# Query projections by row halves from the eighth score on, and three smaller moves of order, in a fused attention and feed-forward block

## The chip, the core and the metric

The kernel runs on one core of one Trainium2 chip. The metric is the device time of one execution in microseconds (us), as the median of several runs.

## What is computed

The reference, cut to its core (one sequence of S = 2048 rows, D = 512, H = 32 heads of 16 columns that share one key and one value head, F = 1792):

```python
def _A_ref(x, wq, wk, wv, wo):
    q = (x @ wq).reshape(B, S, H, Dh).transpose(0, 2, 1, 3)
    k = x @ wk
    v = x @ wv
    scores = jnp.einsum("bhqd,bkd->bhqk", q, k) * (Dh ** -0.5)
    p = _softmax(scores, axis=-1)
    o = jnp.einsum("bhqk,bkd->bhqd", p, v)
    return o.transpose(0, 2, 1, 3).reshape(B, S, H * Dh) @ wo

def _B_ref(x, w_gate, w_up, w_down):
    return (_gelu(x @ w_gate) * (x @ w_up)) @ w_down

h  = x + _A_ref(_layernorm(x), wq, wk, wv, wo)
h2 = h + _B_ref(_layernorm(h), w_gate, w_up, w_down)
```

## The kernel before

**Precision.** Most products are made of three float32r products: both operands are split into a high part and the rest, and high x high, high x rest and rest x high are added in PSUM. A "split" is a cast on one engine and a subtraction on another (`split`, lines 113 to 118).

**Order of the work.** A prologue (line 1206 on) normalises and transposes x, projects keys and values, and makes the first queries. Then come four blocks of 512 queries. Each has eight groups of four heads, each group sixteen slices of 128 keys. A "score" (`score(n)`, line 1006) is two matmuls for two heads, into one of three PSUM buffers, and one exponential of 128 x 1024 on ScalarE (line 395); two scores make a pair, of which four matmuls (`weigh`, line 397) add the weighted values into `acc`. There are 256 scores a block, 1024 in all, counted by n. During block 1 the dense work (output projection, layer norm, feed-forward) of block 0 is woven between the scores, and so on; the dense work of block 3 is a tail without scores.

**What lies in block 0.** Beside the scores of block 0 run the query projections of the other blocks. `project_q(b, cs, ...)` (line 185) makes the queries of block b in chunks c of 128 columns, twelve matmuls each, then splits them (`qh`, `ql`), squares them (`qs`) and stores qh, ql, qh in device memory (`q_d`, line 238). There are two forms. The full form uses all 128 rows of TensorE. The form by halves uses rows 0 to 63 for all twelve terms and then rows 64 to 127: each half matmul runs beside one matmul of a score, which uses the other 64 rows (line 389). Between the two halves of a chunk VectorE reads one column of the bank, a "mark" (line 208), on which TensorE's next half waits. In the form before, the first 32 scores go with full matmuls (chunks 0 and 1 of block 1, and what the prologue left of block 0, `early_q`), taken by steps of three at n = 3, 5, 7 (RAMP) and at every fourth n from 11; from n = 32 on cycles of three scores go with 4 or 2 halves, by a fixed pattern of seven cycles. A chunk in HURRY is first copied out of PSUM (`pq_raw`), so that the bank is free before the split.

**The bound.** For each block the kernel computes a bound of the scores from the squares: a small matmul (`pqn`, line 249), a copy and a maximum on VectorE, four tiny instructions on GpSimd (`factors`, lines 259 to 268), then `m` on VectorE and its store to `q_d` (line 279). These last two steps wait in the list `after`, which `age` counts down once a cycle. At the end of block 0 `check_bound` stores the largest bounds in `b_d` (line 1445).

**GpSimd's other work.** `part_weights` loads the raw weights wo, w_gate, w_up and w_down in 46 parts, splits each on GpSimd, and stores it to device memory; its DMAs go through GpSimd's queue.

**The turn to block 1.** At n = 256 the pool `early`, which held projections and weight parts, is closed, and the pool `dense` takes its memory. At n = 260 `dense(0)` issues on SP's queue, in this order: two tiles of x (`xb`, line 621), four tiles of w1 (line 547), two tiles of wo (`load_wo`, line 561). `evacuate` then copies the last `acc` of block 0 to `oT` (line 412), stores it (`acc_d`, line 416), gathers it back turned (`oc`, line 425), takes reciprocals of the sums, multiplies and splits it (`o_hi`, `o_lo`, lines 439 to 454). The output projection `pp` (`duo`, line 587) needs wo and all four chunks of `o_hi`.

**Whose order is fixed.** In this part the instructions of TensorE, ScalarE, GpSimd, VectorE and SP all stand in the order in which the program emits them. Each engine works through its own list and waits at the head of it.

Of the kernel before, what the change touches and what calls it, by code (L numbers as in the profile page):

```python
# [19 lines left out]
P = 128  # L20
# [16 lines left out]
FULL_Q = 2  # L37

HURRY = ((0, 3), (1, 0), (1, 1))
# [11 lines left out]
def kernel(  # L51
# [104 lines left out]
    def run(outer, first):  # L156
# [28 lines left out]
        def project_q(b, cs, eng, col, halves=()):  # L185
# [4 lines left out]
            for c in cs:  # L190
# [6 lines left out]
                if c in halves:  # L197
                    for a in range(2):
                        rows = slice(64 * a, 64 * a + 64)
                        for n, (lhsT, rhs) in enumerate(terms):  # L200
                            yield a, partial(
                                nc.tensor.matmul, pq, lhsT[rows], rhs[rows],
                                start=(a == 0 and n == 0),
                                stop=(a == 1 and n == len(terms) - 1), skip_group_check=True,
                            )
                        if a == 0:
                            mark = eb.tile([P, 1], F32, tag="qmark", bufs=2, name=f"mark_{b}_{c}")
                            nc.vector.tensor_copy(mark, pq[:, :1])
                else:
                    for n, (lhsT, rhs) in enumerate(terms):  # L210
                        nc.tensor.matmul(  # L211
                            pq, lhsT, rhs, start=(n == 0), stop=(n == len(terms) - 1)
                        )
                        if n % 3 == 2 and (urgent or n < len(terms) - 1):
                            yield 3
# [26 lines left out]
                if c not in halves and (raw is None or b == 0):  # L242
                    yield 3

# [54 lines left out]
        def early_q():  # L299

            second = project_q(1, range(DC), nc.vector, 1, range(FULL_Q, DC))
            for _ in range(sum(RAMP.values())):
                yield next(second)

            next(q_rest)
            for _ in range(FULL_Q * DC - sum(RAMP.values())):
                yield next(second)
            yield from q_rest
            rest_q.append(second)
            rest_q.extend(project_q(b, range(DC), nc.vector, b, range(DC)) for b in range(2, NB))  # L310

        rest_q = []

        def half_q():
            for gen in rest_q:
                yield from gen
# [19 lines left out]
        def first_bound(qg):  # L336

            m = ms[0]
            for u in range(2):
                for a, eng in enumerate((nc.sync, nc.scalar)):  # L340
                    eng.dma_start(
                        qg[64 * a + 3 * DH : 64 * a + 3 * DH + 1, 2 * u + a, :].bitcast(F32),
                        m[2 * u + a : 2 * u + a + 1, :].bitcast(F32),
                    )
            hs = slice(0, FIRST_Q * HC)
            nc.sync.dma_start(q_d[hs, 3 * DH, :T].bitcast(F32), m[hs].bitcast(F32))

# [209 lines left out]
        def load_wo(b):  # L557

            for j in range(DC // 2):
                w = db.tile([P, 2, 2, D], F32R, tag="w2", bufs=W2, name=f"wo_{b}_{j}")  # L560
                nc.sync.dma_start(
# [52 lines left out]
        def dense(b, tail=False):  # L614
# [14 lines left out]
            if b == 0:  # L629
                load_wo(b)  # L630
                yield 0
# [404 lines left out]
        with tc.manual_schedule(engines={mybir.EngineType.SP, mybir.EngineType.DVE}):  # L1036
            parts, said = None, 3
            if first:
                work = early_q()
                parts = part_weights(early.enter_context(tc.tile_pool(name="parts", bufs=1)))  # L1040

            while n < 2 * KC:
                for _ in range(RAMP.get(n, n > 7 and n % 4 == 3) if first else 0):
                    next(work, 0)
                    age()
                score(n)
                n += 1
                if n % 4:
                    continue
                if len(pend) > 2:  # L1050
                    finish(len(pend) - 2)
                if parts is not None and n > 12 and n % 24:
                    next(parts, None)

            token, counts = None, iter(())
            if first:
                drain()
                work = half_q()
                token = next(work)
                counts = (k for _ in range(NB * DC) for k in (4, 2, 4, 2, 4, 4, 4))  # L1060

            for cycle in range((lead - n) // 3):
                age()
                rest = token == REST
                count = next(counts) if token is not None and not rest else 0
                for j in range(3):
                    if n == 2 * PER:
                        assert token is None
                        for _ in parts or ():
                            pass  # L1070
                        while after:
                            age()
# [4 lines left out]
                        db = late.enter_context(tc.tile_pool(name="dense", bufs=1))  # L1077
                    if 0 < j <= count // 2:
                        score(n, (token, next(work)))
                        if j < count // 2:  # L1080
                            token = next(work)
# [8 lines left out]
                ready = [e[2] for e in pend if e[5] < n - 2]  # L1090
                if KC - 1 in ready:
                    ready = ready[: ready.index(KC - 1) + 1]
                finish(len(ready))
                if count:
                    token = next(work, None)
                if outs:
                    take_out()
                if parts is not None and cycle % 7 % 2 == 0:
# [424 lines left out]
```

## Time and profile before

| | us |
|---|---|
| median of three runs | 1439.77 |
| lowest and highest of them | 1437.53, 1440.94 |
| the profiled execution, its own time | 1437.67 |
| span of its instructions | 1436.0 |
| TensorE busy (matmul) | 1400.2 |
| ScalarE busy | 1042.7 |
| VectorE busy | 541.4 |
| GpSimd busy | 231.9 |

The times of all engines below come from one profiled execution, in us from the start of its span. A row of a timeline gives the start, the length, the engine (PE is TensorE, ACT ScalarE, DVE VectorE, POOL GpSimd, SPq SP's queue), the line in the kernel, the operation, what is written and read, how many instructions are merged, and in brackets how long the engine was idle before, and what ended that. A row of a group gives the count, busy us, the mean of one in ns, and the idle time before. A row of waits gives who waited for whom: us in total, times, longest.

### The profile page before, as it was taken

What the parts mean: (1) busy time and instruction counts of PE and PEld (TensorE: products, weight loads), DVE (VectorE), ACT (ScalarE), POOL (GpSimd) and SP (SyncE); (2) the same over time, 40 slices, a digit from 0 to 9 for tenths busy, and PEclk for the clock granted to TensorE, in tenths of its full rate; (3) what the DMA queues carried; (4) which work ended last, traced back from release to release, by engine and by line L of the source; (5) the groups of instructions that cost most, each with busy time, mean ns of one, the idle gap of its engine ahead of it and who ended that gap; (6) DMA issues with size and microseconds to landing.
All of it is one profiled execution on the core that took longest, in us unless ns stands there. A gap on an engine that the chain in (4) does not pass through costs nothing.

```text
span 1436.0 us, 25546 instructions
## 1 busy us (share of the span) xinstructions
PE 1400.2 (98%) x10622; PEld 787.2 (55%) x10622; DVE 541.4 (38%) x974; ACT 1042.7 (73%) x1149; POOL 231.9 (16%) x330
## 2 busy tenths in 40 slices
PE   8999999997999999999999999999999999999998
PEld 7533333334555555555555555554555555557886
DVE  7412231212344242423343342423353242427665
ACT  7699999994778777777777777777787787773000
POOL 6476776730000000000000000000000000002000
PEclk9999999998999999999999999999999999999999
DMA  4567767753144241305243241324143240436551
GB/s 157 161 229 222 226 224 225 235 197 111 48 153 144 74 142 43 132 12 202 60 165 120 86 145 35 117 78 144 57 160 128 86 136 27 146 123 203 177 203 62
DMA packets 71004, 193.69 MB, mean 135 GB/s; under 512 B 9676, under 2 KB 9676, under 8 KB 70848
## 3 DMA queue, kind: packets, MB, share of 16 engines
q1 hardware_dynamic: 60376, 155.69, 32.5%
q0 software_dynamic: 10336, 36.18, 7.6%
q8 instruction: 85, 1.39, 0.4%
q14 instruction: 39, 0.32, 0.1%
q10 hardware_dynamic: 168, 0.10, 0.0%
HBM read 142.12 MB, written 49.55 MB: 133 GB/s over the span
## 4 chain that ended last, share of the span: by engine, by line
PE 87%; ACT 6%; DMA 2%; DVE 2%; issue 1%; SPq 1%; POOL 1%; ACTq 0%; DVEq 0%; POOLq 0%
PE acc L399 30%; PE s L391 19%; PE pu L911 9%; PE pg L911 8%; ACT p L395 6%; PE pd L911 5%; PE pd L587 3%; PE pd L609 3%; PE pg L609 3%; PE pu L609 3%; PE pp L587 2%; PE pq L389 1%; DMA acc_d<-oT 1%; PE pq L211 1%; PE pp L719 1%
## 5 line engine op out<-in xcount | busy, mean ns | idle before, releaser
L395 ACT ACTIVATE p<-s 128x1024 f32<-128x1024 f32 x1024 | 971.2, 1028 | 250.8 <-PE s L391 248.9
L399 PE MATMUL acc<-p,v_sb 128*32 128x512 f32 x4096 | 491.0, 599 | 0.0
L391 PE MATMUL s<-qg,kaug 50*128 50x512 f32 x1984 | 420.2, 426 | 7.6 <-ACT p L395 7.5
L391 PEld LDWEIGHTS s<-qg,kaug 50*128 50x128 f32 x1984 | 192.4, 184 | 254.4 <-ACT p L395 126.5
L399 PEld LDWEIGHTS acc<-p,v_sb 128*32 128x32 f32 x4096 | 112.4, 109 | 235.5 <-issue 230.8
L911 PE MATMUL pu<-x2h,w 64*128 64x512 f32 x672 | 212.2, 391 | 0.0
L911 PE MATMUL pg<-x2h,w 64*128 64x512 f32 x672 | 211.4, 391 | 0.3 <-DVE mark_pg L934 0.3
L911 PEld LDWEIGHTS pu<-x2h,w 64*128 64x128 f32 x672 | 115.9, 185 | 14.9
L911 PEld LDWEIGHTS pg<-x2h,w 64*128 64x128 f32 x672 | 116.0, 185 | 14.5 <-DVE g L785 0.7
L911 PE MATMUL pg<-x2l,w 64*128 64x512 f32 x336 | 122.0, 391 | 0.0
L911 PE MATMUL pu<-x2l,w 64*128 64x512 f32 x336 | 122.0, 391 | 0.0
L127 POOL TENSOR_SCALAR rstd<-mv 128x1 f32<-128x1 f32 x16 | 3.6, 224 | 692.7 <-DVE mv L125 692.6
L788 ACT ACTIVATE ga<-ga 128x512 f32<-128x512 f32 x56 | 35.3, 634 | 89.2 <-DVE ga L783 89.2
L911 PE MATMUL pd<-w,gh 64*128 64x512 f32 x384 | 81.1, 392 | 0.0
L853 DVE TENSOR_TENSOR h<-h,pd 128x512 f32<-128x512 f32 x48 | 31.9, 685 | 115.4 <-PE pd L911 66.3
L439 DVE RECIPROCAL oc<-oc 128x128 f32<-128x128 f32 x64 | 56.3, 921 | 40.4 <-DMA oc<-acc_d 35.5
L1150 DVE SCALAR_TENSOR_TENSOR ga<-ga,g 128x512 f32<-128x512 f32 x70 | 48.3, 691 | 52.7 <-ACT ga L788 51.6
L412 DVE COPY oT<-acc 128x512 f32<-128x512 f32 x32 | 22.1, 691 | 119.0 <-PE acc L399 118.8
L772 DVE COPY g<-pg 128x512 f32<-128x512 f32 x56 | 38.7, 692 | 63.1 <-PE pg L911 57.4
L911 PEld LDWEIGHTS pu<-x2l,w 64*128 64x128 f32 x336 | 58.0, 185 | 7.3
L911 PEld LDWEIGHTS pg<-x2l,w 64*128 64x128 f32 x336 | 58.0, 185 | 6.9
L785 DVE TENSOR_TENSOR g<-g,pu 128x512 f32<-128x512 f32 x56 | 38.3, 684 | 40.2 <-PE pu L911 30.2
(276 smaller groups left out, 1475.3 us busy)
## 6 DMA issues: line engine op xcount, KB each, us to landing
w<-w_d SPq DMA_DIRECT2D x112, 512.0 KB
w<-w_d SPq DMA_DIRECT2D x28, 1024.0 KB
qg<-q_d SPq DMA_DIRECT2D x48, 200.0 KB
q_d<-qh SPq DMA_DIRECT2D x32, 256.0 KB
wo<-wo_d SPq DMA_DIRECT2D x8, 1024.0 KB
acc_d<-oT SPq DMA_DIRECT2D x31, 256.0 KB
oc<-acc_d SPq DMA_DIRECT2D x124, 64.0 KB
w_d<-w_0b POOLq DMA_DIRECT2D x14, 512.0 KB, 4.5
```

Of the source, the lines that this page charges most:

```text
L391: nc.tensor.matmul(s[:, a, :], kaug[rows, kc * P : (kc + 1) * P], qg[rows, 2 * u + a, :], start=True, stop=True,)
L395: nc.scalar.activation(p[:, 2 * u : 2 * u + 2, :], s, AF.Exp, scale=SCALE)
L399: nc.tensor.matmul(acc[32 * j : 32 * j + 32, :], v_sb[:, kc, :], p[:, j, :], start=(kc == 0), stop=(kc == KC - 1), skip_group_check=True,)
L439: nc.vector.reciprocal(oc[:, 1, sl], oc[:, 1, sl])
L587: nc.tensor.matmul(banks[k], lhsT[rows], rhs[rows], start=(turn == 0 and i == 0), stop=(turn == 1 and i == n - 1), skip_group_check=True,)
L609: nc.tensor.matmul(bank, lhsT, rhs, start=(i == 0), stop=(i == len(ts) - 1))
L772: nc.vector.tensor_copy(g, pg)
L785: nc.vector.tensor_tensor(g, g, pu, op=ALU.mult)
L788: nc.scalar.activation(a, a, AF.Tanh, scale=GELU_A * GELU_C)
L853: nc.vector.tensor_tensor(hs[t], hs[t], pd, op=ALU.add)
L911: nc.tensor.matmul(e["bank"], lhsT[rows], rhs[rows], start=i == 0 and not e["both"], stop=last and e["both"], skip_group_check=True,)
L1150: (soon or lazy).pop(0)()
```

## The change

It has four parts.

- The phase with full matmuls ends at n = 8. Of the full form only 18 matmuls of block 1 remain (chunk 0 and half of chunk 1), at n = 3, 5 and 7. From n = 8 on all scores go in cycles of three, with halves beside the second and third score. A cycle takes four halves, or two when the cycle before ended with two weighted sums and the halves are of the upper rows, and never goes past a half's end. The rest of block 0's projection (`q_rest`: the split of chunk 3 and the bound) is emitted at the start of the halves and after chunk (1, 1). At most two pairs are weighed per cycle. Because halves need both row ranges, the first queries `qg` are loaded into both, by two more DMAs on SP behind the store of `m`. Chunk (1, 1) is not in HURRY any more.
- The split of a finished chunk is emitted within the cycle, right after its last half, before the weighted sums and the copy of `acc` that may follow.
- At n = 256 the entries of `after` are emitted before what is left of the weight parts; the parts come in two of three cycles from cycle 3 on.
- `load_wo(0)` is emitted at n = 256, right after the pool is opened, on GpSimd's queue.

The diff, cut:

```diff
-FULL_Q = 2
-HURRY = ((0, 3), (1, 0), (1, 1))
+FULL_STEPS = 18
+HURRY = ((0, 3), (1, 0))
+BREAK = (1, 1)
...
+                for a in range(2) if full <= last else ():
+                    if a or full:
+                        mark = eb.tile([P, 1], F32, tag="qmark", bufs=2, name=f"mark_{b}_{c}_{a}")
+                        nc.vector.tensor_copy(mark, pq[:, :1])
+                    rows = slice(64 * a, 64 * a + 64)
+                    for n, (lhsT, rhs) in list(enumerate(terms))[full:]:
+                        yield a, last - n, partial(nc.tensor.matmul, pq, lhsT[rows], rhs[rows], ...)
...
+        def later_q():
+            second = project_q(1, range(DC), nc.vector, 1, {0: 3 * DC, 1: FULL_STEPS - 3 * DC})
             for _ in range(sum(RAMP.values())):
                 yield next(second)
             next(q_rest)
+            for token in second:
+                if token == HOLD:
+                    yield REST
+                    for _ in q_rest:
+                        pass
+                else:
+                    yield token
+            for b in range(2, NB):
+                yield from project_q(b, range(DC), nc.vector, b, {})
...
             nc.sync.dma_start(q_d[hs, 3 * DH, :T].bitcast(F32), m[hs].bitcast(F32))
+            for a in range(2):
+                nc.sync.dma_start(
+                    qg[64 * a : 64 * a + KR, 1 - a :: 2, :].bitcast(F32),
+                    q_d.rearrange("h r s -> r h s")[:, 1 - a : 4 : 2, :T].bitcast(F32),
+                )
...
-                nc.sync.dma_start(
+                (nc.sync if b else nc.gpsimd).dma_start(
                     w.bitcast(F32),
                     wo_d[2 * j : 2 * j + 2].rearrange("c p i d -> p c i d").bitcast(F32),
...
-            if b == 0:
-                load_wo(b)
...
-            while n < 2 * KC:
-                for _ in range(RAMP.get(n, n > 7 and n % 4 == 3) if first else 0):
+            while n < 2 * PB - 2:
+                for _ in range(RAMP.get(n, 0) if first else 0):
...
-                count = next(counts) if token is not None and not rest else 0
+                count = 0
+                if token is not None and not rest:
+                    count = min(4 if ran < 2 or token[0] == 0 else 2, token[1] + 1)
                 for j in range(3):
                     if n == 2 * PER:
+                        while after:
+                            age()
                         for _ in parts or ():
                             pass
-                        while after:
-                            age()
...
                         db = late.enter_context(tc.tile_pool(name="dense", bufs=1))
+                        load_wo(0)
                     if 0 < j <= count // 2:
-                        score(n, (token, next(work)))
-                        if j < count // 2:
-                            token = next(work)
+                        tokens = token, next(work)
+                        score(n, [(lane, step) for lane, _, step in tokens])
+                        token = next(work, None)
...
-                ready = [e[2] for e in pend if e[5] < n - 2]
+                ready = [e[2] for e in pend if e[5] < n - 2][:2]
...
-                finish(len(ready))
-                if count:
-                    token = next(work, None)
+                ran = len(ready)
+                finish(ran)
...
-                if parts is not None and cycle % 7 % 2 == 0:
+                if parts is not None and cycle > 2 and cycle % 3 < 2:
                     next(parts, None)
```

68 lines of the change are left out of this document (22 added, 46 removed).

## The prediction

> **What bounds the kernel now.** I read the page first, then the exponentials on ScalarE in order of time, then the stretch in which ScalarE and TensorE both fall idle, and last the chain of work that ended last, there. From the page:
>
> ```profile
> span 1436.0 us, 25546 instructions
> ...
> PE 1400.2 (98%) x10622; PEld 787.2 (55%) x10622; DVE 541.4 (38%) x974; ACT 1042.7 (73%) x1149; POOL 231.9 (16%) x330
> ```
>
> TensorE is busy for 98%, but that is an average over two regimes. Query block 0 is paced by the exponentials. ScalarE's timeline shows a group start, its busy time, and the idle time before it:
>
> ```profile
> 61.33 3.77 ACT L395 ACTIVATE p<-s 128x1024 f32<-128x1024 f32 x4 [1.29 <-PE s L391]
> ...
> 85.45 2.86 ACT L395 ACTIVATE p<-s 128x1024 f32<-128x1024 f32 x3 [0.22 <-PE s L391]
> ...
> 91.62 1.94 ACT L395 ACTIVATE p<-s 128x1024 f32<-128x1024 f32 x2 [0.19 <-PE s L391]
> ```
>
> From 61.33 (score 8) to 85.45 (score 32) are 24 scores with full-height projections among them: 1.005 us each, of which 0.94 is the exponential itself (3.77/4). From 85.45 to 91.62 are six scores (two groups of three) with row-half projections: 1.03 us each. So the way of projecting makes almost no difference to the pace.
>
> Block 0 ends in a hole. Two stretches (length, busy of PE, PEld, DVE, ACT, POOL, then the granted clock, the DMA engines' share and GB/s):
>
> ```profile
> 326.00:342.00 16.00, 6.41 (x32) 4.68 (x34) 5.20 (x7) 4.19 (x5) 0.00 (x0) 0.70 0.40 141
> 342.00:358.00 16.00, 16.00 (x122) 8.56 (x120) 4.08 (x9) 9.78 (x11) 1.75 (x4) 0.87 0.10 34
> ```
>
> In the first TensorE works 6.41 of 16 us and the clock falls. Its first dense product there, as a group (count, busy, mean ns, idle before it and what ended that) and in order of time:
>
> ```profile
> L587 PE MATMUL pp<-wo,o_hi 64*128 64x512 f32 x16 | 4.3, 620 | 9.6 <-DVE o_hi L450 7.3 <-DMA wo<-wo_d 2.3
> ```
>
> ```profile
> 333.09 0.43 PE L391 MATMUL s<-qg,kaug 50*128 50x512 f32 x2
> ...
> 340.79 1.22 PE L587 MATMUL pp<-wo,o_hi 64*128 64x512 f32 x4 [7.28 <-DVE o_hi L450]
> ```
>
> It waits 2.3 us for wo and then 7.3 us for the last quarter of the attention output, o_hi. What makes o_hi late stands in SP's queue and in the chain that ended last (start, length):
>
> ```profile
> 314.74 0.82 SPq L621 DMA_DIRECT2D xb<-in_A_x_dram  x2
> 315.62 3.11 SPq L547 DMA_DIRECT2D w<-w_d  x4
> 318.77 1.14 SPq L561 DMA_DIRECT2D wo<-wo_d  x2
> 320.01 0.46 SPq L416 DMA_DIRECT2D acc_d<-oT  x1
> ```
>
> ```profile
> 309.11 4.91 DMA b_d<-q2m
> 320.01 12.44 DMA acc_d<-oT
> 333.79 2.15 DMA oc<-acc_d
> 336.16 3.40 DVE oc L439 x4
> ```
>
> Sizes of one transfer, from the page's part 6:
>
> ```profile
> w<-w_d SPq DMA_DIRECT2D x112, 512.0 KB
> ...
> wo<-wo_d SPq DMA_DIRECT2D x8, 1024.0 KB
> acc_d<-oT SPq DMA_DIRECT2D x31, 256.0 KB
> ```
>
> The store b_d (each head's largest bound, for the flag) must land before the old pool's memory is free; only then SP issues two xb (tiles of acc_d's size), four w and two wo, 0.5 + 2.0 + 2.0 MB, and behind them the 0.25 MB of acc_d, which lands 12.44 us after its issue. Then come the gather, four reciprocals, multiply and cast. **So the end of the hole, 340.8, is set by b_d and by the bytes ahead of acc_d, not by how fast block 0 computes.** Without both waits (2.3 and 7.3), and with some 1.2 us less for matmuls at the reduced clock, TensorE would stand at the o_hi matmul at 333.09 + 0.43 - 2.3 - 1.2 = 330.0: block 0 has 10.8 us of slack. Behind the hole the instruction orders of TensorE, ScalarE and VectorE are the same in both kernels.
>
> **The change, part by part.** The profiled execution took 1437.67 us (span 1436.0 and 1.67 around it); the median of the three runs, 1439.77, lies 2.10 above. I sum against the first and add the 2.10.
>
> *1. Halves from pair 8 (a loss inside block 0).* Only 18 full-height matmuls of block 1 are left; chunk 1 of block 1 is finished by halves beside score 9 and later. Its first half waits on a new mark on VectorE, and VectorE's order is fixed: the mark stands behind the split of block 0's chunk 3.
>
> ```profile
> 62.57 0.43 DVE L117 CAST qh<-pq_raw 128x512 fp32r<-128x512 f32 x1 [3.95 <-issue]
> ...
> 63.64 1.58 DVE L233 TENSOR_TENSOR qs<-qh 128x512 bf16<-128x512 f32 x1
> ```
>
> That split waits 3.95 us for its buffer, that is for chunk 2's stores to land, and ends at 63.64 + 1.58 = 65.22. The mark, a copy of one column, then ends near 65.4 if nothing else moves. But SP gets two more loads, which wait until the store of m has landed:
>
> ```profile
> 48.15 0.51 SPq L346 DMA_DIRECT2D q_d<-m  x1
> 48.71 0.69 SPq L238 DMA_DIRECT2D q_d<-qh  x1
> ...
> 53.50 1.71 SPq L238 DMA_DIRECT2D q_d<-qh  x1
> ```
>
> All stores of chunks 1 and 2 (48.71 to 53.50) queue behind them. The shift lies between 0 (they are bound by transfer anyway) and the 4.8 us that those stores span; I take the middle, 2.4. The mark then ends at 67.8; about 0.6 for two halves, the score and its latency (a guess between 0.3 and 1.0 from the 0.43 row above) puts exponential 9 at 68.4. It would have begun at 61.33 + 0.94 = 62.3. **Stall 6.1 us** (3.7 to 8.5). The matmuls of it, six halves more in all, lie under the exponentials: 0; without that cover a pair would cost 0.43.
>
> *2. The split at once.* It is emitted ahead of the copy of acc instead of behind it. Twice TensorE waited for it (total, times, longest):
>
> ```profile
> PE pq L389 <- DVE ql L118: 3.4, 2, 1.7
> ```
>
> ScalarE has up to half a microsecond of scores in store each time, so of 3.4 us I count 2.4 as saved. Against it, four halves now always fall in the cycle that ends with two weighted sums, and the three-score form runs 24 scores longer (24 x 0.025 = 0.6). I take both to cancel (-2.4 to +3). TensorE thus stands at the o_hi matmul at 330.0 + 6.1 = 336.1, still ahead of 340.8: the stall is hidden by the hole.
>
> *3. The bound's factors on GpSimd.* GpSimd works in order: weight parts, with the four factor instructions between them.
>
> ```profile
> 72.16 0.26 POOL L259 TENSOR_SCALAR mm<-q,k2m 32x1 f32<-32x1 f32 x1 [5.78 <-DVE q L254]
> ...
> 87.54 0.61 POOL L117 CAST w_0b<-w_0r 128x512 fp32r<-128x512 f32 x1 [4.46 <-DMA w_0r<-in_B_w_gate_dram]
> ```
>
> ```profile
> 130.41 0.26 POOL L259 TENSOR_SCALAR mm<-q,k2m 32x1 f32<-32x1 f32 x1 [1.44 <-ACT p L395]
> ```
>
> ```profile
> POOL mm L259 <- DVE q L254: 8.7, 3, 5.8
> ```
>
> ```profile
> 308.01 0.75 POOL L511 DMA_DIRECT2D w_d<-w213b  x1
> ```
>
> The first factors (72.16) belong to block 0's remaining chunks. Their sums now come after score 22 instead of score 19, and 6.1 us later in time: about 9.7 us. Of that, the 4.46 us in which GpSimd waited for a weight load swallow their part: 5.2 left. The later factors meet a late GpSimd and wait no more (1.44 at 130.41, and 8.7 - 5.8 = 2.9 in the two others: 4.3): 0.9 left. In the built order the last weight part's store still comes before the last factors, contrary to the change's words, and now even its issue does: + 1.0 (0.75 and a gap). But b_d then lands with that 512 KB store mostly done: 4.91 becomes some 3.4 (between 2.0, nearest the gather's 2.15, and 4.91). Sum: +0.4 on the start of xb and w1.
>
> *4. wo on GpSimd's queue.* It starts with xb, not after w1. SP issues acc_d 1.1 us sooner, but every byte ahead of it is still on its way, over the same DMA engines. Bounds: 0, and wo's part of the 17.7 us between 314.74 and the landing at 332.45 (2.0 of 4.75 MB: -7.5). No row of before has two full-width streams at once; I take -0.7, near the end at which only the issue counts. [...]
>
> *5. Clock.* After the hole 16 us ran at 0.87, a loss of 2.1 us. With TensorE idle for 4 us in place of 9.6, I take 0.8 of it back (0 to 2.1).
>
> Sum: +0.4 - 0.7 - 0.8 = -1.1 us: 1436.6 for an execution like the profiled one, **1438.7** beside the median.
>
> **Rivals.** *B, faster:* acc_d gets past wo (another queue, served first). For it: wo leaves SP's queue. Against: the bytes are the same. Term 4 is then -7.5, o_hi would be ready near 333.6, and TensorE's own arrival at 336.1 decides: 340.8 becomes 336.5 (-4.3), and the clock loss goes (-2.1): 1433.4.
>
> *C, slower:* the late first factors carry through all weight parts, because the loads behind them come as much later. Then 4.46 swallows nothing: 9.7 - 4.3 + 1.0 = +6.4 on b_d, and on the end of the hole: 1446.2. It decides as soon as over 2 us of the lateness survive. For it: GpSimd has one order, and its loads are issued from that order. Against: weight loads waited with 4.46 us to spare.
>
> *D, nothing:* the stores land as early as now, the halves cost and bring nothing: 1439.8.
>
> **How the numbers follow.** A (forecast) 0.38, its own range 1436.3 to 1442; B 0.27; C 0.29; D 0.06. A measurement of this kernel tells about 0.2% (2.9 us) from no change. Faster by more: B and 0.04 of A, 0.31. Slower by more: C and 0.03 of A, 0.32. Within: 0.37. The range reaches to B and C, 1433 to 1446.
>
> **What would show it.** Step 1: an idle of about 6 us before exponential 9, ended by a mark. Step 2: no projection waits for ql. Step 3: b_d issued near 311. Step 4: acc_d landing about 17 us after the first xb. The hole: TensorE waits once, some 4 us, for o_hi. I am wrong if TensorE reaches the hole after o_hi is ready, or if the hole is gone.

## The result and the profile after

The changed kernel takes **1443.8 us** in the median of 22 runs (1436.09 to 1449.98); the kernel before takes 1439.62 in 22 runs beside them (1437.53 to 1441.64). The ratio is 1.0029, with a 95% interval from 1.0017 to 1.004: slower by 0.3%, where I had forecast 1438.7, 1.1 us less than before. The time lies outside the forecast's own range (1436.3 to 1442) and inside the whole one (1433 to 1446). Two things stand out at once: it is slower, and its runs spread over 14 us where those of before spread over 4.

The profiled execution of the changed kernel took 1445.67 us, 8.0 more than that of before. The medians differ by 4.2: with a spread of 14 us one execution is a draw. I read the trace for where the time arises, and the medians for how much it is. From the page:

```profile
span 1444.0 us, 25562 instructions
...
PE 1406.6 (97%) x10628; PEld 789.6 (55%) x10628; DVE 542.3 (38%) x975; ACT 1041.9 (72%) x1149; POOL 231.3 (16%) x332
```

TensorE's busy time grew by 6.4 us with almost the same matmuls. From exponential 8 to 32 it was busy for 27.16 us (61.28 to 96.67, 183 matmuls, mean granted clock 0.86), where before took 21.96 (61.33 to 85.45, 157 matmuls, clock 1.00); a part of these 5.2 us is work at half clock, as the windows below show. First the stall of step 1, on ScalarE's timeline (start, busy, idle before it and what ended that) and on VectorE's:

```profile
61.28 1.02 ACT L404 ACTIVATE p<-s 128x1024 f32<-128x1024 f32 x1 [1.29 <-PE s L400]
70.66 1.94 ACT L404 ACTIVATE p<-s 128x1024 f32<-128x1024 f32 x2 [8.36 <-PE s L400]
75.52 2.86 ACT L404 ACTIVATE p<-s 128x1024 f32<-128x1024 f32 x3 [2.92 <-PE s L400]
...
96.67 3.77 ACT L404 ACTIVATE p<-s 128x1024 f32<-128x1024 f32 x4 [0.45 <-PE s L400]
```

```profile
66.52 0.43 DVE L119 CAST qh<-pq_raw 128x512 fp32r<-128x512 f32 x1 [3.95 <-DMA q_d<-qh]
66.98 1.63 DVE L120 TENSOR_TENSOR ql<-pq_raw,qh 128x512 fp32r<-128x512 f32 x1
68.53 0.68 DVE L237 TENSOR_TENSOR qs<-qh 128x512 bf16<-128x512 f32 x1
69.14 0.14 DVE L212 COPY mark<-pq 128x1 f32<-128x1 f32 x1
```

The split of block 0's chunk 3 waits for its buffer until 66.52, and the mark ends at 69.28. Exponential 9 begins at 70.66. Behind it there is a second idle of 2.92 us, and exponential 32 stands at 96.67 where it stood at 85.45: 11.2 us late. The windows (length, busy time of PE, PEld, DVE, ACT, POOL, then granted clock, DMA share, GB/s) show where the 2.92 comes from, and the same thing again at the end of block 0:

```profile
65.00:75.00 10.00, 5.67 (x26) 1.99 (x26) 2.73 (x4) 1.94 (x2) 2.98 (x4) 0.50 0.67 234
...
345.00:354.80 9.80, 5.50 (x26) 2.29 (x30) 5.03 (x8) 1.94 (x2) 0.00 (x0) 0.50 0.07 22
```

TensorE idled for 8.12 us, the granted clock fell to 0.50, and the first work behind the stall ran at that clock: sixteen matmuls of `weigh` took 3.64 us from 71.41, and 1.92 us from 76.11, at a clock of 1.00. The stretches at 0.50 (the one at the program's end left aside) run from 329.1 to 332.5 and from 335.9 to 346.2 us before, and from 64.8 to 75.0 and from 344.6 to 354.9 after. They add up to 13.7 us before and 20.5 us after.

TensorE's waits (total, times, longest) name the two that count:

```profile
PE pp L596 <- DVE o_hi L459: 8.4, 1, 8.4
PE pq L398 <- DVE mark L212: 8.1, 1, 8.1
```

There is no wait for ql any more. Now the first factors of each remaining chunk's bound, on GpSimd:

```profile
87.41 0.26 POOL L265 TENSOR_SCALAR mm<-q,k2m 32x1 f32<-32x1 f32 x1 [19.35 <-DVE q L260]
133.87 0.25 POOL L265 TENSOR_SCALAR mm<-q,k2m 32x1 f32<-32x1 f32 x1
237.68 0.26 POOL L265 TENSOR_SCALAR mm<-q,k2m 32x1 f32<-32x1 f32 x1
```

Before, they stood at 72.16, 130.41 and 218.36 (the last ones at 306.44), and GpSimd came to each of them before its data did. Now it waits 19.35 us for the first, and for no later one. The end of block 0, in order of time:

```profile
317.20 0.63 POOL L520 DMA_DIRECT2D w_d<-w213b  x1 [0.30 <-POOL w213b L120]
317.93 0.26 POOL L265 TENSOR_SCALAR mm<-q,k2m 32x1 f32<-32x1 f32 x1
319.58 0.53 DVE L281 TENSOR_SCALAR m<-qn,mm 32x512 fp32r<-32x512 f32 x1 [11.61 <-POOL mm L274]
320.59 0.36 SPq L1443 DMA_DIRECT2D b_d<-q2m  x1
323.97 1.38 SPq L630 DMA_DIRECT2D xb<-in_A_x_dram  x2
...
338.08 0.74 PE L596 MATMUL pp<-wo,o_hi 64*128 64x512 f32 x4 [0.25 <-DMA w<-w_d]
...
341.06 1.73 SPq L434 DMA_DIRECT2D oc<-acc_d  x4
...
349.31 1.22 PE L596 MATMUL pp<-wo,o_hi 64*128 64x512 f32 x4 [8.37 <-DVE o_hi L459]
```

The order is what counts here. TensorE comes to this product at 338.08, in time for the 340.79 of before. But the last factors wait behind the last weight part, b_d is issued 11.5 us later than before (309.11), xb 9.2 later (314.74), the gather oc 8.6 later (332.47), and o_hi 8.5 later (340.79). The span is 8.0 longer. So the stall did not reach the end through TensorE. It reached it through GpSimd.

### The profile page after: what moved, and what is told of

The parts are those of the page before. It is cut to its first block, busy times and chain, and to the rows that moved or that the text cites. A ratio compares the mean times of both kernels' runs of the same rounds, so it can differ in the third digit from the quotient of the medians.

```text
span 1444.0 us, 25562 instructions
## 1 busy us (share of the span) xinstructions
PE 1406.6 (97%) x10628; PEld 789.6 (55%) x10628; DVE 542.3 (38%) x975; ACT 1041.9 (72%) x1149; POOL 231.3 (16%) x332
## 4 chain that ended last, share of the span: by engine, by line
PE 86%; ACT 6%; DMA 3%; DVE 2%; issue 1%; SPq 1%; POOL 0%; ACTq 0%; DVEq 0%; POOLq 0%
PE acc L408 30%; PE s L400 18%; PE pu L919 10%; PE pg L919 7%; ACT p L404 6%; PE pd L919 4%; PE pd L596 3%; PE pd L618 3%; PE pg L618 3%; PE pu L618 3%; PE pq L398 2%; PE pp L596 2%; DMA acc_d<-oT 1%; PE pp L727 1%; DMA q_d<-qh 1%
## 5 line engine op out<-in xcount | busy, mean ns | idle before, releaser
L919 PEld LDWEIGHTS pg<-x2h,w 64*128 64x128 f32 x672 | 116.0, 185 | 11.5 <-DVE h L861 0.2
```

The costliest lines, as they stand in the source:

```text
L919: nc.tensor.matmul(e["bank"], lhsT[rows], rhs[rows], start=i == 0 and not e["both"], stop=last and e["both"], skip_group_check=True,)
```

## The experiments

Theory **T**: late first factors delay GpSimd's weight parts, these delay b_d, and the end follows the start of xb. Rivals: **R1**, TensorE's own late block 0 decides; **R2**, wo's move or the two extra loads cost the time. Later came **T2**, theory T with the reason that GpSimd has no slack left behind the late first factors, so that its waits for weight loads set b_d; **R3**, that these loads are bound by transfer and not by latency; and **R4**, the denser issue of the weight parts. All times below are medians; each kernel is measured against the kernel before in runs beside it, whose median lay between 1439.4 and 1440.2.

**One part alone, or undone.**

*e4_wo_sync*: the changed kernel with wo back on SP's queue.

```
-                (nc.sync if b else nc.gpsimd).dma_start(
+                nc.sync.dma_start(
...
+                load_wo(b)          # behind w1, as before
-                        load_wo(0)
```

> The changed kernel with wo loaded by SP's queue behind w1, as before (part 4 undone). Theory T: two streams share the 16 DMA engines, so only the issue time comes back: acc_d lands 0.6 to 1.1 us later after the first xb, and the time is 0.6 to 1.1 us above the changed kernel's (ratio 1.003 to 1.004). Rival B (acc_d passes wo on the other queue): 4 to 7 us slower than the changed kernel (ratio 1.006 to 1.008). Rival R2 (wo on GpSimd's queue costs time, because it competes with w1): 1 to 5 us faster.

Measured 1442.99 (1439.07 to 1448.05), ratio 1.0026 [1.0014, 1.0039]. That is 0.8 below the changed kernel, well inside its spread: rival B is out, and a term under 1 us can't be told here.

*e5_before_wo*: the kernel before with only wo on GpSimd's queue (the same edit, the other way round).

> The kernel before, with only wo loaded by GpSimd's queue at score 256 (part 4 alone). [...] Rival B (acc_d passes wo): -4 to -7.5 us. Rival R2 (the second queue costs time): slower by 1 us or more.

Measured 1439.58, ratio 0.9991 [0.9982, 1.0]. From its timeline:

```profile
314.40 0.82 SPq L621 DMA_DIRECT2D xb<-in_A_x_dram  x2
314.76 1.45 POOL L561 DMA_DIRECT2D wo<-wo_d  x2 [6.00 <-PE s L391]
330.88 1.73 SPq L425 DMA_DIRECT2D oc<-acc_d  x4
```

From xb to the gather are 16.48 us, where before had 332.47 - 314.74 = 17.73: 1.25 saved in this trace (forecast in term 4: 0.7), 0.6 in the medians, where the interval reaches to no change. B is out and R2 with it, as far as it speaks of wo.

*e6_before_loads*: the kernel before with only the two loads of qg behind the store of m.

```
             nc.sync.dma_start(q_d[hs, 3 * DH, :T].bitcast(F32), m[hs].bitcast(F32))
+            for a in range(2):
+                nc.sync.dma_start(
+                    qg[64 * a : 64 * a + KR, 1 - a :: 2, :].bitcast(F32),
...
```

> The kernel before, with only the two extra loads of qg that wait for the store of m on SP's queue (a redundant load of the same data). Forecast of step 1: they shift the stores of chunks 1 and 2 by about 2.4 us (0 to 4.8), the split of block 0's chunk 3 ends 2 to 4 us later than 65.2; no mark of chunk (1,1) stands behind it here, so block 0 goes on and the time stays within 1 us of before (1439 to 1441). If the loads themselves are what costs the time: 1442 or more.

Measured 1439.59, ratio 0.9994 [0.9986, 1.0003]: no cost by themselves. The split of chunk 3 began at 66.82 (before 62.57), so the loads shift it by 4.25, near the upper end of my 0 to 4.8. No mark stands behind that split here, so nothing waits for it. R2 falls.

*e13_before_rate*: the kernel before with the denser issue of the weight parts alone. The prediction had not priced this line at all.

```
-                if parts is not None and cycle % 7 % 2 == 0:
+                if parts is not None and cycle % 3 < 2:
```

> The kernel before, with the weight parts issued in two cycles of three as in the changed kernel, instead of four of seven. It tells which part of the change takes GpSimd's slack: T2 says the late first factors (the stall), so here the last part ends within 2 us of before and the time stays 1439 to 1441 with a spread near 4 us. Rival R4 (the denser issue puts more parts ahead of the factors, VectorE's m and with it the splits come late, and this costs the time): 1442 to 1445 with a spread over 8 us.

Measured **1452.51** (1446.98 to 1458.88), ratio 1.0088 [1.0065, 1.011]. My expectation failed by 12 us, and R4 was right in sign and too small. The rows of chunk 2's factors:

```profile
242.46 0.25 POOL L259 TENSOR_SCALAR mm<-q,k2m 32x1 f32<-32x1 f32 x1
...
244.11 0.79 DVE L275 TENSOR_SCALAR m<-qn,mm 32x512 fp32r<-32x512 f32 x1 [23.11 <-POOL mm L268]
244.83 0.14 DVE L208 COPY mark<-pq 128x1 f32<-128x1 f32 x1
...
245.02 0.79 PE L389 MATMUL pq<-xT_hi,wq_hi 64*128 64x512 f32 x1 [12.75 <-DVE mark L208]
```

Parts are issued every 4.5 scores instead of 5.25, but from the first factors on GpSimd takes some 5.2 us for one (44 parts in 230 us, 72.16 to 302.40). The program therefore runs ahead of GpSimd, and a factor that is issued at its usual score stands behind more parts: 34 instead of 30 for chunk 2 (32 in the changed kernel). It comes 24.1 us later than before (218.36). VectorE's order is fixed, so m waits 23.1 us, the mark behind m waits with it, and TensorE behind the mark. This is the same kind of stall as at exponential 9, in the middle of block 0.

The changed kernel has that risk as well. In its profiled execution chunk 2's m waited 9.9 us and ended just ahead of TensorE's need; in e4_wo_sync's, which differs in wo alone, it did not:

```profile
242.87 0.79 DVE L281 TENSOR_SCALAR m<-qn,mm 32x512 fp32r<-32x512 f32 x1 [14.40 <-POOL mm L274]
...
245.04 0.79 PE L398 MATMUL pq<-xT_hi,wq_hi 64*128 64x512 f32 x1 [4.29 <-DVE ql L120]
```

**The end follows the start of xb.** *e7_late_factors*: the kernel before with added work on GpSimd (a memset and eight multiplications of a tile that nothing reads).

```
                         for _ in parts or ():
                             pass
+                        if first:
+                            scrap = eb.tile([P, 512], F32, name="scrap")
+                            nc.gpsimd.memset(scrap, 1.0)
+                            for _ in range(8):
+                                nc.gpsimd.tensor_scalar(scrap, scrap, 1.0, None, op0=ALU.mult)
```

> The kernel before, with work added: a memset and eight multiplications of one 128x512 tile on GpSimd between the last weight part and the last bound's factors (about 9 x 0.6 = 5 to 6 us; nothing else reads the tile). Theory T (the end of the kernel follows the issue of b_d one for one, since o_hi waits for the transfers behind it): b_d is issued 5 to 6 us later, o_hi comes as much later, and the time rises by 5 to 6 us (ratio 1.0035 to 1.004), with nothing changed in block 0's pace. Rival R1 (TensorE's arrival decides, b_d has slack): no change, ratio 1.000.

Measured 1444.62 (1443.34 to 1446.29), ratio 1.0031 [1.002, 1.0042]. The added work ran behind the factors, not ahead of them, and took longer than I had thought:

```profile
310.88 0.66 SPq L1450 DMA_DIRECT2D b_d<-q2m  x1
310.97 12.51 POOL L1075 TENSOR_SCALAR scrap<-scrap 128x512 f32<-128x512 f32 x8
323.50 0.83 SPq L621 DMA_DIRECT2D xb<-in_A_x_dram  x2
...
340.49 1.74 SPq L425 DMA_DIRECT2D oc<-acc_d  x4
```

b_d itself is only 1.8 late. But the old pool's memory is free only when its last user on GpSimd is done, at 323.48, and xb starts at 323.50: 8.8 later than before, the gather 8.0 later, the span 8.0 longer (1444.0). So it is not b_d alone that counts. It is whatever of the old pool ends last, b_d or GpSimd's own last work. The pace of block 0 is untouched here, which speaks against R1 for the kernel before. In the medians the 8.0 are 4.5: before's profiled execution is among the shortest of its runs.

*e3_parts_early*: the changed kernel, where GpSimd may work parts during the stall.

```
-                if parts is not None and cycle > 2 and cycle % 3 < 2:
+                if parts is not None and cycle % 3 < 2:
```

> The changed kernel, but GpSimd's weight parts may be taken from the first cycle on, not from the fourth, so that GpSimd works on parts while TensorE and ScalarE stand in the stall before exponential 9. The stall itself is untouched. Theory T: the wait for the mark stays near 8 us and score 256 stays near 322 us, but the last weight part and with it b_d come 7 to 10 us sooner (310 to 313), o_hi is ready near 341, where TensorE itself arrives (338 to 341), and the time falls by 6 to 8 us, to ratio 0.998 to 1.000. Rival R1 (TensorE's late block 0 decides by itself): no change, ratio 1.003, whatever b_d does. This run tells T from R1.

Measured 1442.12, ratio 1.0019 [1.001, 1.0027]: 1.7 below the changed kernel instead of 6 to 8. The last part was split 13.8 us sooner (301.83), but 34 parts now stood ahead of chunk 2's factors, and TensorE stood 5.6 us before exponential 177. It came to o_hi's product only at 342.88 and did not wait for o_hi. One delay was traded for another, the first sign of R4.

*e14_sparse* and *e15_early_sparse*: the changed kernel with the parts in four cycles of seven, from the fourth cycle on and from the first.

```
-                if parts is not None and cycle > 2 and cycle % 3 < 2:
+                if parts is not None and cycle > 2 and cycle % 7 % 2 == 0:   # e14
+                if parts is not None and cycle % 7 % 2 == 0:                 # e15
```

> The changed kernel with the weight parts issued in four cycles of seven from the fourth cycle on, instead of two of three; the stall before exponential 9 stays. Theory S (the stall alone makes GpSimd late; the denser issue only adds to the wait of VectorE's m): the first factors stay near 87 us, b_d near 318 to 321, the time within 2 us of the changed kernel (1442 to 1446). Theory D (the denser issue, which puts 34 parts instead of some 31 ahead of chunk 2's factors, costs the larger share): VectorE's m of chunk 2 no longer waits 9.9 us, and the time falls by 3 us or more, to 1437 to 1441.

> The changed kernel with the weight parts from the first cycle on and in four cycles of seven; the stall stays. GpSimd then works parts during the stall and has fewer of them ahead of chunk 2's factors. If GpSimd's order is all that the stall touches: TensorE's arrival decides as in e10_two_ahead, 1434 to 1437 in the median, that is 5 us below e3_parts_early (1442.1), which differs from it in the denser issue alone. If the stall itself costs more: 1440 or over.

Measured 1449.0 (1446.3 to 1453.66), ratio 1.0059 [1.0043, 1.0076], and 1440.34, ratio 1.001 [0.9994, 1.0025]. In e14 both theories failed. In e15 the first expectation failed (1434 to 1437), and the other (1440 or over) holds by 0.3 us. In e14 m of chunk 2 no longer waits, but the work has only moved to the end:

```profile
307.76 0.26 POOL L265 TENSOR_SCALAR mm<-q,k2m 32x1 f32<-32x1 f32 x1 [3.75 <-DVE q L260]
310.68 0.63 SPq L1443 DMA_DIRECT2D b_d<-q2m  x1
...
323.54 0.62 POOL L520 DMA_DIRECT2D w_d<-w213b  x1 [0.30 <-POOL w213b L120]
327.25 1.07 SPq L630 DMA_DIRECT2D xb<-in_A_x_dram  x2
```

b_d goes out at 310.68, near the 309.11 of before. Three parts are left behind the last factors, and xb waits for the last one's store. So the question "the stall or the denser issue" was put wrongly: GpSimd has 45 parts to do here behind the first factors, which took it 235 us (87.19 to 321.97), and when it starts at 87 instead of 72 neither order of issue makes up for that. Dense issue makes the factors late (chunk 2's by 24.1 us in e13), sparse issue makes the parts late (the last one's store is issued at 323.54 in e14, 317.20 in the changed kernel). In e15 it starts sooner (three parts are done before the first factors, not two), and 3.5 us of the changed kernel's time go. With the stall in place the sparse issue alone thus costs 5.2 us (e14 against the changed kernel), and with the early start it saves 1.8 us (e15 against e3, whose intervals overlap). So the 12.3 us of e13 can't be carried over to the changed kernel.

**The root of the stall.** *e1_mark_first* and, again, *e16_mark_again*: the changed kernel with the mark ahead of chunk 3's split in VectorE's order. *e2_qbufs3* and *e17_qbufs_again*: three buffers for the split's outputs, so that it needn't wait for chunk 2's stores.

```
             next(q_rest)
+            yield next(second)                                              # e1, e16
...
-                qh = eb.tile([P, T], F32R, tag="qh", bufs=2, name=f"qh_{b}_{c}")
+                qh = eb.tile([P, T], F32R, tag="qh", bufs=3, name=f"qh_{b}_{c}")   # e2, e17; ql alike
```

> The changed kernel, but in VectorE's order the first mark of chunk (1,1) stands ahead of the split of block 0's chunk 3 instead of behind it, so the halves no longer wait for the stores of chunk 2. Theory T (the stall before exponential 9 delays the first bound's factors, GpSimd's in-order weight parts carry that to the issue of b_d, and the end of the kernel follows b_d): the wait of TensorE for the mark falls from 8.1 us to under 1, the first factors come near 77 us instead of 87.4, b_d is issued near 312 to 314 instead of 320.6, and the profiled time is 6 to 9 us below the changed kernel's 1445.7, that is ratio 0.998 to 1.000 to the kernel before. Rival R1 (the stall goes straight to the end through TensorE's own order): the same -8 to -9 in time, so this run tests the root and not the path; exponential 33 comes 9 us sooner under both. Rival R2 (wo's move or the two extra loads cost the time): no change, ratio 1.003.

> The changed kernel, but the split's outputs qh and ql have three buffers instead of two, so that the split of block 0's chunk 3 waits for the stores of chunk 1 (landed at 60.8 us in the changed kernel) and not for those of chunk 2 (66.4). Step 1 of the prediction named that buffer as the cause of the stall. If it is: the mark ends near 63, TensorE's wait for it falls from 8.1 us to 1 to 2, the first factors come near 79 and the time is that of e1_mark_first within 2 us (1438 to 1442). If something else holds the split (the stall stays over 6 us), no change: 1443 to 1445.

> e1_mark_first again (first mark ahead of the split of block 0's chunk 3), beside e2_qbufs3 on one chip. If its 1440.1 was this kernel's own: 1438 to 1442, and 5 us or more above e17_qbufs_again. If it came of the chip or of chance in twelve runs with a spread of 13 us: within 3 us of e17_qbufs_again.

> e2_qbufs3 again (three buffers for the split's outputs). If its 1433.7 was this kernel's own: 1432 to 1436. If it came of the chip or of chance: 1436 to 1440, as e16_mark_again within 3 us.

Measured: 1440.06 and 1440.17 with the mark first (ratios 0.9997 [0.9983, 1.0011] and 0.9988 [0.9974, 1.0002]); 1433.73 and 1437.26 with three buffers (0.9965 [0.995, 0.998] and 0.9976 [0.9964, 0.9988]). Both take the wait for the mark from 8.1 to some 1 us, so step 1 had the cause right. The medians of e1 and e16 lie in their ranges; e2 lies 4 us below its own, and e17 in the range that stood for chance. Both kinds gain less than the 11 us of the stall, and both still spread over 10 to 13 us. A part of what is missing shows in all four traces: TensorE now waits 2.8 to 4.5 us for chunk 2's ql before exponential 177, the kind of wait that e13 showed, which the changed kernel's own trace does not have. The buffers are better by 6.3 us in the first pair, measured on two chips, and by 2.9 in the second, on one chip; by the sign set beforehand (within 3 us) the larger gap came of the chip or of chance. A smaller gain is likely but not shown, since the intervals of the second pair overlap. The first factors come 1 to 3 us sooner with the buffers (77.7 and 77.3, against 78.7 and 80.3).

**GpSimd's slack.** In all kernels so far GpSimd loads a part's weights just one part ahead. From its first factors to the last part the changed kernel's GpSimd waits 45.0 us for such loads in all, before's 43.9. *e10_two_ahead*: the changed kernel, loads two parts ahead; stall and issue untouched.

```
-                raw = pw.tile([P, D], F32, tag="w_raw", bufs=2, name=f"{name}r")
+                raw = pw.tile([P, D], F32, tag="w_raw", bufs=3, name=f"{name}r")
...
-                if i + 1 < len(steps):
-                    raws[i + 1] = steps[i + 1][0]()
+                if i + 2 < len(steps):
+                    raws[i + 2] = steps[i + 2][0]()
```

> The changed kernel, but GpSimd loads the raw weights two parts ahead instead of one (three buffers instead of two); the stall before exponential 9 and the order of the parts are untouched. In the changed kernel GpSimd waits some 45 us in all for these loads between 60 and 318 us, and behind the first factors it waits for nothing else. Theory T2 (T, sharpened: behind the late first factors GpSimd has no slack left, so its weight parts with their load waits set b_d, and the length of these waits, which differs from run to run, makes the spread of the changed kernel): the load waits shrink by 20 us or more, GpSimd again waits for q at the later factors, b_d is issued near 311 to 313 instead of 320.6, TensorE's own arrival near 338 to 341 decides, the time falls by 4 to 7 us in the median (ratio 0.998 to 1.000) and its spread from 14 us to about 5. Rival R1 (TensorE's late block 0 decides by itself): no change, 1.003. Rival R3 (the loads are bound by transfer and not by latency): the waits stay, no change.

Measured **1434.02** (1433.01 to 1434.74), ratio 0.9966 [0.9953, 0.9979], against 1.0029 of the changed kernel: 9.8 us less, where T2 expected 4 to 7, and a spread of 1.7 us (over five runs only). GpSimd's waits and the end of block 0:

```profile
POOL mm L265 <- DVE q L260: 27.4, 3, 18.6
...
POOL w_1b L119 <- DMA w_d<-w211b: 5.3, 1, 5.3
```

```profile
306.59 0.26 POOL L265 TENSOR_SCALAR mm<-q,k2m 32x1 f32<-32x1 f32 x1 [7.08 <-DVE q L260]
309.25 0.36 SPq L1443 DMA_DIRECT2D b_d<-q2m  x1
312.66 1.97 SPq L630 DMA_DIRECT2D xb<-in_A_x_dram  x2
328.91 1.93 SPq L434 DMA_DIRECT2D oc<-acc_d  x4
...
336.58 0.72 PE L596 MATMUL pp<-wo,o_hi 64*128 64x512 f32 x4 [0.25 <-issue]
```

The waits for loads are gone (what is left waits for the stores of earlier parts, a kind that was hidden), and GpSimd waits for q again, 7.08 us at the last factors: it has slack. The stall before exponential 9 is still there in full (8.4 us for the mark), and TensorE comes to o_hi's product at 336.58 without a wait. o_hi is ready at 337.3, before TensorE reaches the product of its last quarter at 339.2. Here, as in e3 and not in the changed kernel, R1 holds: TensorE's own lateness decides. Rival R3 falls.

*e9_mark_rate* (mark first, parts from the first cycle, four cycles of seven) and *e11_mark_two_ahead* (mark first and loads two ahead):

> The changed kernel with the first mark ahead of the split, the weight parts from the first cycle on, and in four cycles of seven as before the change instead of two of three, so that the parts are not issued faster than GpSimd works them and fewer stand in front of a factor. T2: the factors no longer wait behind a backlog, so VectorE's m of chunk 2's bound is not late and TensorE does not stand before exponential 177 (2.6 to 5.8 us in the runs so far); b_d near 305 to 309, the time 1431 to 1436 in the median, spread under 8 us. If the rate is without effect: as e1_mark_first, 1440.

> The changed kernel with both the first mark ahead of the split of block 0's chunk 3 (as in e1_mark_first) and the raw weights loaded two parts ahead. T2: neither TensorE nor GpSimd is late; b_d near 307 to 309, the time 1429 to 1434 in the median (ratio 0.993 to 0.996) with a spread of some 5 us: faster than both kernels. R1: the same 1431 to 1434, since the stall is gone. R3: as e1_mark_first, 1440 in the median with a spread of 13 us.

Measured 1435.13 (1431.52 to 1445.88), ratio 0.9975 [0.996, 0.999], and **1427.34** (1426.24 to 1427.95), ratio 0.9916 [0.9903, 0.9928]. The first falls where it was expected, though with a spread of 14 us (one run at 1445.88, the others within 6); as its GpSimd waits for q again, lost slack alone does not explain every spread. The second is faster than both kernels, 2 us below its own range, and 6.7 below e10: what the stall costs once no hole hides it.

*e12_before_two_ahead*: the kernel before, loads two ahead.

> The kernel before, with the raw weights loaded two parts ahead (three buffers instead of two) and nothing else of the change. In the kernel before GpSimd waits 8.7 us for q at three factors and reaches the last ones with 2.3 us to spare, so its parts hardly set b_d. T2: b_d stays within 2 us of 309.1, but the last part's store no longer runs beside it, so the start of xb and w1 comes up to 3 us sooner; the time falls by 0 to 4 us, to 1436 to 1440. That would leave 6 to 11 us between this kernel and the changed one with the same loads and the early mark (1427.3), as what the change is worth once GpSimd has slack. If before's own hole was made by GpSimd's load waits too: 1429 to 1434.

Measured 1439.57, ratio 0.9997 [0.9988, 1.0005]: no gain. Its GpSimd reaches the last factors 9.76 us early instead of 2.3, but the last part's store is issued behind them, at 309.57, and xb starts at 316.28, no sooner than before. From the first factors to the last part its waits for loads fall from 43.9 to 1.9 us, but 29.1 us of waits for stores and 11.9 us of waits for q (2.1 before) stand there instead, and GpSimd is just 5.4 us sooner through. So with the same loads the change as it stands is worth 1434.02 - 1439.57 = -5.6 us, and with the early mark -12.2 (-4.7 and -11.4, if each is taken against the kernel before beside it).

The path in numbers, from the profiled execution of twelve kernels: issue of the first xb, of the gather oc, span, and the difference of the last two.

| kernel | xb | oc | span | span - oc |
|---|---|---|---|---|
| e11 mark first, two ahead | 307.15 | 323.37 | 1426.2 | 1102.8 |
| e1 mark first | 311.97 | 328.67 | 1429.3 | 1100.6 |
| e2 three buffers | 312.54 | 328.74 | 1429.8 | 1101.1 |
| e10 two ahead | 312.66 | 328.91 | 1431.3 | 1102.4 |
| e5 before, wo | 314.40 | 330.88 | 1434.3 | 1103.4 |
| before | 314.74 | 332.47 | 1436.0 | 1103.5 |
| e3 parts early | 319.25 | 335.52 | 1438.4 | 1102.9 |
| e4 wo on SP | 322.79 | 339.93 | 1441.8 | 1101.9 |
| e7 before, late work | 323.50 | 340.49 | 1444.0 | 1103.5 |
| changed | 323.97 | 341.06 | 1444.0 | 1102.9 |
| e14 sparse | 327.25 | 344.17 | 1447.9 | 1103.7 |
| e13 before, dense | 330.33 | 347.28 | 1450.4 | 1103.1 |

Over 23 us of xb's start the remainder moves by 3. (The other six traces, e6, e9, e12, e15, e16 and e17, have remainders from 1102.3 to 1104.0.) In eight of the twelve TensorE waits for o_hi. In e2, e3, e10 and e11 it doesn't: there it comes to the last quarter of o_hi up to 2.1 us after that is ready, so its own arrival decides, and moves with xb.

## Why the prediction was wrong

**What bounds the kernel: right.** The end of the hole is set by what frees the old pool and by the bytes ahead of acc_d (from xb to the gather pass 16.2 to 17.7 us in the twelve kernels of the last table; before, the DMA engines move 400 GB/s from 321 to 329 us, at a share of 1.02). e7, where only the start of xb was moved, shows it, and the last table agrees for the eight kernels in which TensorE waits for o_hi; "I am wrong if the hole is gone" did not occur in the changed kernel. But I named b_d alone; e7 and e14 show that GpSimd's last store or instruction counts as well.

**Step 1, mechanism right, size off.** The stall stands where I put it and is ended by the mark. I took 6.1 us (3.7 to 8.5); it was 8.36 + 2.92 = 11.3. The stores shifted the split by 3.95 us instead of 2.4, from the mark's end to exponential 9 passed 1.38 us instead of 0.6, and I had left out the granted clock, which was 0.50 behind this stall until 75.0 us. (The split itself took no longer: 2.69 us from the start of qh to the end of qs, 2.65 before.) "Hidden by the hole" was right for TensorE alone, which was there at 338.08.

**Step 2, right.** The waits for ql are gone, and from exponential 32 to 256 the kernel before needs 225.76 us and the changed one 225.54: a net of -0.2, where I had 0.

**Step 3 failed**, at "the later factors meet a late GpSimd and wait no more: 0.9 left". The first factors came 15.25 us late (forecast 9.7, of which the stall makes 11.2 and the later score 4.05, forecast 3.6). At the part whose load wait of 4.46 us was to swallow its share GpSimd is 11.13 us late (98.67 instead of 87.54): 4.1 swallowed. These 11.1 us should have shrunk by the 4.3 of later waits for q, of which 2.06 stand ahead of the last part and 2.26 behind it, at the last factors. The waits did vanish, but the last part was split only at 315.63 instead of 302.40, 13.2 late. What I had left out are the other waits for loads. Behind that part they are 43.7 us instead of 39.4, as if the slack had only changed its place. The load of the very last part is one piece of it (first before, then after):

```profile
300.15 1.49 POOL L500 TENSOR_SCALAR w213r<-w213r 128x512 f32<-128x512 f32 x1 [0.94 <-DMA w213r<-in_B_w_down_dram]
```

```profile
313.38 1.49 POOL L509 TENSOR_SCALAR w213r<-w213r 128x512 f32<-128x512 f32 x1 [4.57 <-DMA w213r<-in_B_w_down_dram]
```

A wait that vanishes is no time gained if another wait lay beside it. My reading is that while GpSimd waited for q before, the load of its next part was on its way, and that without that wait the load is waited for instead. Wait by wait this isn't shown, and load waits also differ between executions: in e5, e6 and e7, where GpSimd does the same up to the last part as in the kernel before, they are 44.3 to 45.3 us in all, instead of 43.9. What is shown is that the loads close the chain: in e10, with the loads out of the way, the waits for q come back, b_d is issued at 309.25, and the change is 9.8 us faster. I also did not price the denser issue at all, although the line stood in the diff; e13 puts it at +12.3 us in the kernel before, but in the changed kernel the old rate is no faster (e14).

b_d's landing went the way it was forecast: from its issue to xb are 3.38 us instead of 5.63, -2.25 (forecast -1.5).

**Step 4, right.** From xb to the gather are 17.09 us instead of 17.73: -0.64, forecast -0.7; e5 alone gave -1.25 in its trace and -0.6 in the medians. SP's issue of wo took 1.14 us before: the -0.64 and the -0.6 lie within that, the -1.25 just outside. With both queues at work the DMA engines moved 417 GB/s at a share of 1.03 (the changed kernel, 330 to 336 us), with SP's alone 400 at 1.02 (before, 321 to 329 us), so the second queue brought little more throughput.

**Step 5 wrong with step 3.** TensorE waited 8.4 us for o_hi, not 4, and the granted clock fell to 0.50 again (344.6 to 354.9 us).

**The rivals.** C came nearest: late factors carried through the weight parts to b_d. I gave it 0.29 and 1446.2 for the median, 1444.1 for an execution like the profiled one; measured were 1443.8 and 1445.67. But its sum is not what happened, and that the number fits is partly luck. In C the 4.46 us swallow nothing and the 4.3 of later waits still count, which makes b_d 6.4 us late; in the trace 4.1 were swallowed, what the later waits gave the loads took back, and b_d was 11.5 late, of which its shorter landing gave back 2.25. Against C I had set the load slack. It was there, and too little.

## What to carry to other kernels

The slack of an engine that works in order is not the sum of its waits: when one kind is taken away, another can appear in its place, as in e12, where 42 us less of load waits made GpSimd 5.4 us faster. Small instructions that others wait for, queued behind long ones on such an engine, are priced by what stands ahead of them (in e13 chunk 2's factors stood behind 34 parts instead of 30 and came 24.1 us later), so every change of how densely the long ones are issued is a change of their time. A spread that grows from 4 to 14 us was here the sign of a chain that had lost its slack to transfers (1.7 us with the loads two ahead); look for such a chain before looking for single microseconds.

## What the runs showed of the hardware

- One multiplication of a 128x512 f32 tile by a constant takes 12.51/8 = 1.56 us on GpSimd. I had estimated 0.6 from its cast of that size (0.61); the halving of the weight parts (1.50) was the row to take.
- wo on a second queue beside xb and w1 saved 0.64 us (the changed kernel) and 1.25 us (e5) of 17.73 in the traces, and 0.6 in the medians of e5, which is not clear of noise.
- Behind TensorE's wait of 8.1 us came another 2.92 us of idle on ScalarE. From 70 to 75 us TensorE was busy throughout at a granted clock of 0.50, where one matmul of a score took 0.62 us (0.39 at 75.3, at a clock of 1.00): scores came too slowly for ScalarE.
